# Seven block products instead of eight in the feed-forward stage, and the order of every engine written out, in a fused attention and SwiGLU kernel

## The chip, the core and the metric

The kernel runs on one core of a Trainium2 chip. The metric is the device time of one execution in microseconds, the median of several runs. Five engines work side by side: PE (TensorE, matrix products), DVE (VectorE), ACT (ScalarE), POOL (GpSimd) and SP (SyncE, which here only issues DMAs). PE writes to PSUM, which has eight banks of 128 partitions by 512 floats; the other tiles lie in SBUF.

## The reference: attention, then a gated feed-forward layer

All in 32-bit floats on 8 sequences of 448 tokens, with 12 heads of 64 (768 features):

```python
q_n, k_n = rmsnorm(q, g_q), rmsnorm(k, g_k)          # over the 64 of a head
attn = softmax(q_n @ k_n.T / sqrt(64)) @ v           # 8 x 12 x 448 x 64
x = attn.transpose(0, 2, 1, 3).reshape(3584, 768)
xn = x / sqrt(mean(x * x, -1) + 1e-6) * rms_g
g, val = xn @ w_gate, xn @ w_val                     # 768 x 1536 each
out = (g * sigmoid(g) * val) @ w_out                 # 1536 x 768
```

The weights arrive as 64-bit floats, two 32-bit words to a number, and are brought to 32 bits on the chip.

## The kernel before

The function `safe_scores` does all the work that is timed (`any_scores` stands behind a flag that large gains would set). A sequence is worked on as six pairs of heads, 48 pairs in all, and then as a feed-forward part (FFN).

**A pair.** `load_pair` fetches q, k and v. `norm_pair` takes squares on ACT (L460), sums them on DVE (L463), and has POOL make the reciprocal root by a power (L466) and scale q (L468). `turn(g, 0)` and `turn(g, 1)` transpose q and k on PE (L482, tile `tr`) and copy them out by ACT (L485) and DVE (L487). `score` makes scores of keys by queries (L497, tile `sc`, four PSUM banks) and their exponentials on ACT (L501). `values` multiplies by v (L519, tile `av`) and sums the exponentials over keys by a product with ones (L526, tile `den`); from the second sequence on POOL adds the four key tiles first (L507, L511, tile `es`). `divide` takes the reciprocal on DVE (L535), multiplies (L540), and adds the squares into `ss` (L545, L546).

**The end of a sequence.** `rms_x` sums `ss` over features on PE (L558, tile `msx`), POOL takes the power (L562), and `norm_x` spreads it by a product (L568, tile `rb`) and scales x on DVE (L571).

**The FFN.** `project` multiplies x with a 128-column block of a weight: six products of 128x128 by 448 tokens (L578, tile `ff`, two PSUM banks). `gate` follows with a tanh on ACT (L585) and one DVE instruction (L587), `val` with one more (L593), whose result is a row block of `hT`. `project_out` makes 128 tokens by 384 features with twelve products (L603). The output weights stay in SBUF; blocks of the gate and value weights are fetched again for each sequence from a 32-bit copy in DRAM (`kept`), three blocks ahead. In the first sequence each block is converted once by `convert`, 768 numbers a partition at a time: two ACT instructions (L413, L419), two of POOL (L414, L420), two of DVE (L416, L417).

**The order.** `fill` deals the FFN of sequence b in 24 slots over the pairs of sequence b+1, in proportion to its cost, and keeps `LEFT` = 2 items for the time in which the next x is normed. The first sequence's six pairs have no FFN beside them, and the last sequence's FFN has no pairs. A scheduler then sets each engine's order by its own priorities; the text is a hint.

In the trace a 32-bit product shows as two MATMUL and two LDWEIGHTS (weight load) records; "product" below is one call in the text, "record" one of the trace.

Of the kernel before, what the change touches and what calls it, by code (L numbers as in the profile page):

```python
# [23 lines left out]
HALF = DM // 2  # L24
CW = 512
# [307 lines left out]
def safe_scores(  # L333
# [15 lines left out]

    nc = tc.nc  # L350
# [3 lines left out]

    const, small = pool("c_const", 1), pool("c_small", 4)
    qk_pool, v_pool, qn_pool, qkT_pool = pool("c_qk", 3), pool("c_v", 3), pool("c_qn", 1), pool("c_qkT", 2)
    e_pool, tmp, y_pool = pool("c_e", 13), pool("c_tmp", 8), pool("c_y", 2)
    xT_pool, w_pool = pool("c_xT", 2), pool("c_w", 3)
    raw_pool, cv_pool = pool("c_raw", 3), pool("c_cv", 2)
# [16 lines left out]
    gqk = const.tile([128, 1], F32, name="gqk")  # L376
    nc.vector.scalar_tensor_tensor(gqk, gq, 1.0 / D**0.5, gk, ALU.mult, ALU.mult)

    nc.vector.tensor_scalar(gqk, gqk, SAFE / D, -SAFE / D, ALU.min, ALU.max)
# [7 lines left out]
    nc.vector.tensor_tensor(row[:, 0, :], row[:, 0, :], row[:, 1, :], ALU.mult)  # L387
    top = const.tile([1, 1], F32, name="top")
    nc.vector.tensor_reduce(out=top, in_=row[:, 0, :], axis=AX_X, op=ALU.max, apply_absolute_value=True)
    nc.vector.tensor_scalar(flag, top, 8.0, SAFE, ALU.mult, ALU.is_gt)  # L390

    wo = const.tile([128, NFC, DM], F32, name="wo")
    hT = const.tile([128, NFC, 512], F32, name="hT")
    st = {}


    kept = {w: scratch.tile([NFC, 128, DM], F32, name=f"kept_{w}") for w in "gv"}
    W_AHEAD = 3

    def convert(dst, src):  # L400

        if src.dtype == F32:
            nc.sync.dma_start(out=dst, in_=src)
            return
        a, n = src.shape[1], src.shape[2]
        assert a * n == DM
        raw = raw_pool.tile([128, 2 * DM], I32, name="raw")
        nc.sync.dma_start(out=raw.rearrange("p (a n w) -> p a (n w)", a=a, w=2).bitcast(I64), in_=src)
        words = raw.rearrange("p (n w) -> p n w", w=2)
        lo, hi = words[:, :, 0], words[:, :, 1]  # L410
        top = cv_pool.tile([128, DM], I32, name="top")

        nc.scalar.activation(top.bitcast(F32), hi.bitcast(F32), ACT.Abs)  # L413
        nc.gpsimd.tensor_scalar(top.bitcast(F32), top.bitcast(F32), 122879.9921875, 2.0**-15, ALU.min, ALU.max)  # L414

        nc.vector.tensor_scalar(top, top, 3, 0x3FFFFFF8, ALU.logical_shift_left, ALU.bitwise_and)  # L416
        nc.vector.scalar_tensor_tensor(top, hi, -(2**30), top, ALU.bitwise_and, ALU.bitwise_or)  # L417

        nc.scalar.activation(lo, lo.bitcast(U32), ACT.Copy, scale=2.0**-29)  # L419
        nc.gpsimd.tensor_tensor(dst.rearrange("p a n -> p (a n)").bitcast(I32), top, lo, ALU.add)  # L420

    def weight(w, n):

        if n >= B * NFC:
            return
        b, fc = divmod(n, NFC)
        t = st["w", w, n] = w_pool.tile([128, NDC, 128], F32, name=f"w{w}", tag=f"w{w}")
        if b == 0:
            src = {"g": moe_w_gate, "v": moe_w_val}[w]
            convert(t, src[:, fc * 128:(fc + 1) * 128].rearrange("(c p) f -> p c f", p=128))  # L430
            nc.sync.dma_start(out=kept[w][fc], in_=t.rearrange("p c f -> p (c f)"))
        else:
            nc.sync.dma_start(out=t.rearrange("p c f -> p (c f)"), in_=kept[w][fc])
# [299 lines left out]
```

## Time and profile before

| | us |
|---|---|
| three runs | 1847.08, 1847.25, 1849.09 (median 1847.25) |
| the profiled execution | 1850.28 |
| its span, first to last instruction | 1848.4 |
| mean granted PE clock over the span | 0.982 |
| busy PE / DVE / ACT / POOL | 1778.2 / 510.6 / 441.8 / 638.1 |
| first product of `rms_x` for sequences 0, 1 and 7 | 132.3, 358.6, 1654.2 |
| DMA | 149 MB, 153,280 packets on the main queue, 27.6% of 16 engines |

The span falls into four parts: the first 14 us without products, the first sequence's pairs up to 132 us, the steady part, and the last FFN from 1654 us. A profile row names the line, engine, operation, tiles as out<-in, partitions by elements, and the count; then busy time and mean duration, or start and length.

### The profile page before, as it was taken

The numbers are of one execution on the slowest core, as the hardware profiler recorded it, in microseconds if no ns is written. First come the engines' busy times: TensorE is split into PE (matmuls) and PEld (weight loads), VectorE is DVE, ScalarE is ACT, GpSimd is POOL, SyncE is SP. The second block draws the span as 40 slices with busy tenths as digits, with TensorE's granted clock in tenths as the row PEclk, the third lists the DMA queues.
The fourth block names the chain that finished last, engine by engine and source line by source line (L and its number), as shares of the span: only waits on it lengthen the run. The fifth ranks groups of instructions, "written<-read, shape, count | busy, mean of one in ns | idle before, by whom it ended". The sixth has DMA issues, their size and how long they took to land. (4 is left out here: it accounts for less than half of the span.)

```text
span 1848.4 us, 15816 instructions
## 1 busy us (share of the span) xinstructions
PE 1778.2 (96%) x5960; PEld 880.4 (48%) x5960; DVE 510.6 (28%) x546; ACT 441.8 (24%) x725; POOL 638.1 (35%) x527
## 2 busy tenths in 40 slices
PE   5878989999999999999999999999999999999998
PEld 2333434544455444554455544554445544455554
DVE  3646664122212222123212222222221222111100
ACT  5643442122121313112221122212222122210000
POOL 6765774324232424322432243323234133210000
PEclk9888999999999999999999999999999999999999
DMA  5625653122220323113321232212231132202200
GB/s 157 219 76 156 194 190 99 32 82 80 87 55 27 90 83 93 46 53 88 87 65 38 66 91 83 68 41 84 84 90 41 41 87 67 69 18 74 88 9 28
DMA packets 154475, 149.00 MB, mean 81 GB/s; under 512 B 95509, under 2 KB 124693, under 8 KB 154389
## 3 DMA queue, kind: packets, MB, share of 16 engines
q1 hardware_dynamic: 153280, 147.88, 27.6%
q8 instruction: 50, 0.82, 0.2%
q14 instruction: 37, 0.29, 0.1%
q10 hardware_dynamic: 1108, 0.00, 0.0%
HBM read 127.41 MB, written 20.45 MB: 80 GB/s over the span
## 5 line engine op out<-in xcount | busy, mean ns | idle before, releaser
L578 PE MATMUL ff<-xT,wg 128*128 128x448 f32 x1152 | 457.0, 547 | 7.3 <-DVE ga L587 7.2
L578 PE MATMUL ff<-xT,wv 128*128 128x448 f32 x1152 | 456.6, 546 | 3.4 <-DVE hT L593 3.4
L603 PE MATMUL ff<-wo,hT 128*128 128x384 f32 x1344 | 444.6, 488 | 0.0
L603 PEld LDWEIGHTS ff<-wo,hT 128*128 128x128 f32 x1344 | 251.6, 190 | 182.2 <-issue 14.9
L578 PEld LDWEIGHTS ff<-xT,wg 128*128 128x128 f32 x1152 | 215.7, 191 | 231.6 <-issue 212.0
L578 PEld LDWEIGHTS ff<-xT,wv 128*128 128x128 f32 x1152 | 214.3, 191 | 229.6 <-issue 215.3
L511 POOL TENSOR_TENSOR es<-es,e 112x448 f32<-112x448 f32 x168 | 187.0, 1145 | 289.3 <-ACT e L501 289.3
L501 ACT ACTIVATE e<-sc,rs 112x448 f32<-112x448 f32 x384 | 214.2, 636 | 160.8 <-PE sc L497 160.7
L497 PE MATMUL sc<-qkT 64*112 64x448 f32 x768 | 185.4, 590 | 21.8 <-DVE qkT L487 15.2
L546 POOL TENSOR_TENSOR ss<-ss,s 128x448 f32<-128x448 f32 x40 | 46.6, 1164 | 427.4 <-ACT s L545 427.4
L535 DVE RECIPROCAL rd<-den 128x448 f32<-128x448 f32 x48 | 141.9, 2956 | 180.6 <-PE den L526 180.6
L519 PE MATMUL av<-e,vt 112*64 112x448 f32 x768 | 159.1, 557 | 0.0
L466 POOL TENSOR_TENSOR rs<-ms,mhalf 112x16 f32<-112x16 f32 x48 | 140.4, 2926 | 4.0
L585 ACT ACTIVATE th<-ff 128x448 f32<-128x448 f32 x96 | 52.0, 541 | 342.5 <-PE ff L578 342.4
L587 DVE SCALAR_TENSOR_TENSOR ga<-th,ff 128x448 f32<-128x448 f32 x96 | 59.2, 617 | 252.8 <-ACT th L585 252.8
L593 DVE SCALAR_TENSOR_TENSOR hT<-ga,ff 128x448 f32<-128x448 f32 x96 | 59.3, 618 | 236.5 <-PE ff L578 232.6
L463 DVE TENSOR_REDUCE ms<-sq 112x16 f32<-112x1024 f32 x48 | 58.5, 1219 | 216.8 <-ACT sq L460 201.2
L497 PEld LDWEIGHTS sc<-qkT 64*112 64x112 f32 x768 | 66.7, 180 | 104.4 <-issue 58.0
L507 POOL TENSOR_TENSOR es<-e 112x448 f32<-112x448 f32 x84 | 94.1, 1140 | 50.7 <-ACT e L501 50.7
L545 ACT ACTIVATE s<-xT 128x448 f32<-128x448 f32 x40 | 23.1, 577 | 327.7 <-DVE xT L540 327.7
L519 PEld LDWEIGHTS av<-e,vt 112*64 112x64 f32 x768 | 52.0, 140 | 97.7 <-issue 97.4
L468 POOL TENSOR_TENSOR qn<-qk,rs 112x512 f32<-112x512 f32 x48 | 51.4, 1070 | 80.8 <-PE tr L482 79.8
(46 smaller groups left out, 709.9 us busy)
## 6 DMA issues: line engine op xcount, KB each, us to landing
wg<-kept_g SPq DMA_DIRECT2D x84, 384.0 KB, 3.0
wv<-kept_v SPq DMA_DIRECT2D x84, 384.0 KB, 3.0
qk<-in_q_dram SPq DMA_DIRECT2D x96, 112.0 KB, 3.3
qk<-in_k_dram SPq DMA_DIRECT2D x96, 112.0 KB, 3.2
vt<-in_v_dram SPq DMA_DIRECT2D x48, 224.0 KB, 2.6
raw<-in_moe_w_gate_dram SPq DMA_DIRECT2D x12, 768.0 KB, 5.9
raw<-in_moe_w_val_dram SPq DMA_DIRECT2D x12, 768.0 KB, 4.8
raw<-in_moe_w_out_dram SPq DMA_DIRECT2D x12, 768.0 KB, 4.5
```

The costliest lines, as they stand in the source:

```text
L463: nc.vector.tensor_reduce(out=ms, in_=sq.rearrange("p (n d) -> p n d", d=D), axis=AX_X, op=ALU.add)
L466: nc.gpsimd.tensor_tensor(rs, ms, mhalf[0:P, :], ALU.pow)
L497: nc.tensor.matmul(ps, lhsT=qkT[r, 1, c * P:(c + 1) * P], rhs=qkT[r, 0, :], start=True, stop=True)
L501: nc.scalar.activation(e, ps, ACT.Exp, scale=rs[:, n:n + 1])
L507: nc.gpsimd.tensor_tensor(es, st["e", g, 0, j], st["e", g, 1, j], ALU.add)
L511: nc.gpsimd.tensor_tensor(es, es, st["e", g, c, j], ALU.add)
L519: nc.tensor.matmul(av[j * D:(j + 1) * D, 0:S], lhsT=vt[:, j, c, :], rhs=st["e", g, c, j], start=(c == 0), stop=(c == NT - 1))
L535: nc.vector.reciprocal(rd, den[:, 0:S])
L578: nc.tensor.matmul(ps, lhsT=wt[:, c, :], rhs=st["xT", b][:, c, :], start=(c == 0), stop=(c == NDC - 1))
L587: nc.vector.scalar_tensor_tensor(ga, th, 1.0, g, ALU.add, ALU.mult)
L593: nc.vector.scalar_tensor_tensor(hT[:, fc, c0:c0 + S], st.pop(("ga", b, fc)), 0.5, st.pop(("v", b, fc)), ALU.mult, ALU.mult)
L603: nc.tensor.matmul(ps, lhsT=hT[:, fc, i * 128:(i + 1) * 128], rhs=wo[:, fc, n * HALF:(n + 1) * HALF], start=(fc == 0), stop=(fc == NFC - 1))
```

## The change

`safe_scores` is rewritten. The sums below hold for one pair of FFN column blocks (`fp` and `fp + 6`), once for gate and once for value.

**Products.** The 448 tokens and the 768 features of x are halved, which gives A11 to A22 of 224 tokens by 384 features; the weight is halved into B11 to B22 of 384 by 128. Instead of eight products A·B there are seven, of A11, A12, A22 or the sums S1 to S4 with B11, B21, B22 or T1 to T4 (Strassen's scheme in Winograd's form). One `product` is two weights by three 128x128 blocks by 224 tokens, gate and value side by side in one bank. `quad` does the seven for one `fp`, and adds them up on DVE from PSUM (`plus`: u2, u3, c22, c21, c12); `hand` does the tanh and two DVE instructions for each of three parts. Two products are accumulated onto a bank that already holds one (`onto`). PSUM is now four banks for scores, one for `av` and later transposes, and three (`ps_f`) for the FFN.

**Sums.** `norm_x` makes S1 to S4 once a sequence: four DVE instructions of 128x672. T1 to T4 are made once, in the first sequence, by 48 DVE instructions of 128x384.

**Weights.** All blocks are 128x384: 72 to convert, and 84 blocks of the seven kinds plus 24 of the output weight, kept in DRAM and fetched for each later sequence into a ring of 24, up to 20 ahead. Conversion goes in turns: turn n loads piece n, splits piece n-2, joins piece n-3 and makes the T of piece n-4. There are three turns a pair while the first sequence's pairs are alone, then one with each FFN item.

**Order.** `manual_schedule` leaves every engine in the order of the text; `after(n, ...)` puts an instruction of another engine behind the n-th next PE step. FFN items now are 42 products and 18 or 24 thirds of an output tile, dealt in 27 slots, with 7 left for the norm. A pair's squares are two instructions, and q is loaded by one DMA in place of two.

PE while the first sequence's pairs are alone, one pair before and after (`qn` is q, `qk` is k):

```order
L497 MATMUL sc<-qkT 112x448 x4
L482 MATMUL tr<-ident,qn 128x112 x4
L519 MATMUL av<-e,vt 64x448 x8
L526 MATMUL den<-e,ones 64x448 x7
L482 MATMUL tr<-ident,qk 128x112 x4
```

```order
L469 MATMUL sc<-qkT 112x448 x4
L454 MATMUL tr<-ident,qn 128x112 x4
L454 MATMUL tr<-ident,qk 128x112 x4
L494 MATMUL av<-e,vt 64x448 x8
L469 MATMUL sc<-qkT 112x448 x4
L506 MATMUL den<-e,ones 64x448 x8
```

The transposes of k have moved ahead of `av`, and the second half of the scores ahead of `den`.

DVE during the first sequence's FFN, before and after (`top` is a weight being converted, `wt` a T block, `u_`, `cc` and `c_` the sums of products):

```order
L535 RECIPROCAL rd<-den 128x448
L540 TENSOR_TENSOR xT<-av,rd 128x448
L416 TENSOR_SCALAR top<-top 128x768
L417 SCALAR_TENSOR_TENSOR top<-raw,top 128x768
L593 SCALAR_TENSOR_TENSOR hT<-ga,ff 128x448
L487 COPY qkT<-tr 128x448
```

```order
L698 TENSOR_TENSOR u_1780<-ff,u_1725 128x448
L604 TENSOR_SCALAR top<-top 128x384
L605 SCALAR_TENSOR_TENSOR top<-raw,top 128x384
L650 TENSOR_TENSOR wt<-wt 128x384 x3
L698 TENSOR_TENSOR cc<-ff,u_1780 128x448
L426 TENSOR_REDUCE ms<-sq 112x8
L510 RECIPROCAL rd<-den 128x448
L517 TENSOR_TENSOR x<-av,rd 128x448
L698 TENSOR_TENSOR c_1839<-ff,u_1780 128x448
```

A sum of products, which PE waits for before it uses a bank again, now stands between conversions, T sums and a reciprocal.

PE in the steady part, from a `den` to the next scores, before and after (in the second with tile numbers, which show the bank):

```order
L526 MATMUL den<-es,ones 64x448 x2
L603 MATMUL ff<-wo,hT 128x384 x12
L482 MATMUL tr<-ident,qk 128x112 x4
L497 MATMUL sc<-qkT 112x448 x8
L603 MATMUL ff<-wo,hT 128x384 x12
```

```order
L506 MATMUL den_3015<-es_2690,ones_136 64x448
L686 MATMUL ff_3030<-x_1197,wt_2845 128x224 x3
L686 MATMUL ff_3030<-x_1197,wt_2848 128x224 x3
L686 MATMUL ff_3043<-xs_2833,wt_2851 128x224 x3
L686 MATMUL ff_3043<-xs_2833,wt_2854 128x224 x3
L454 MATMUL tr_3057<-ident_131,qk_2645 128x112 x4
L686 MATMUL ff_3030<-x_2201,wt_2857 128x224 x3
L686 MATMUL ff_3030<-x_2201,wt_2860 128x224 x3
L686 MATMUL ff_3079<-x_1197,wt_2870 128x224 x3
L686 MATMUL ff_3079<-x_1197,wt_2875 128x224 x3
L469 MATMUL sc_3094<-qkT_2697 112x448
```

Two FFN products stand between `den` and the transposes of k, two between those and the scores; the third product goes onto the bank of the first (`ff_3030`).

The core of the diff:

```diff
-    ps_s, ps_m, ps_f = pool("c_ps_s", 4, space=PSUM), pool("c_ps_m", 2, space=PSUM), pool("c_ps_f", 2, space=PSUM)
+    ps_s, ps_m, ps_f = pool("c_ps_s", 4, space=PSUM), pool("c_ps_m", 1, space=PSUM), pool("c_ps_f", 3, space=PSUM)
+    ctx.enter_context(tc.manual_schedule(engines={E.PE, E.Activation, E.DVE, E.Pool, E.SP}))
...
+    def after(n, fn):
+        due.append((now["t"] + n, fn))
...
+        op("S1", "A21", "A22", ALU.add)
+        op("S2", "S1", "A11", ALU.subtract)
+        op("S3", "A11", "A21", ALU.subtract)
+        op("S4", "A12", "S2", ALU.subtract)
...
+    def convert(upto=None):
...
+        if 0 <= n - 3 < len(pieces):
+            key = pieces[n - 3][0]
+            st[key] = block()
+            join(*st.pop(("cv", n - 3)), st[key][0])
...
+            sums = {"B12": (("T1", "B12", "B11"), ("T2", "B22", "T1"), ("T3", "B22", "B12")), "B21": (("T4", "B21", "T2"),)}
...
+    def product(b, fp, left, right, onto=None):
+
+        bank = ps_f.tile([128, 512], F32, name="ff", tag="f") if onto is None else onto
+        x = st["left", b][left]
+        for w in range(2):
+            wt = st["w", b, fp, right, w][0]
+            for c in range(3):
+                nc.tensor.matmul(bank[:, w * HT:(w + 1) * HT], lhsT=wt[:, c * 128:(c + 1) * 128], rhs=x[:, c, :],
+                                 start=onto is None and w == c == 0, stop=c == 2, skip_group_check=True)
+            used(("w", b, fp, right, w))
+        return bank
+
+    def quad(b, fp):
...
+        def plus(name, ps, other, dst=None):
+            add[name] = tmp.tile([128, S], F32, name=name, tag=name, bufs=1) if dst is None else dst
+            nc.vector.tensor_tensor(add[name], ps[:, 0:S], add[other], ALU.add)
+
+        def hand(gate, value, dst):
...
+            nc.scalar.activation(th, gate, ACT.Tanh, scale=0.5)
+
+            def rest():
+                nc.vector.scalar_tensor_tensor(dst, th, 1.0, gate, ALU.add, ALU.mult)
+                nc.vector.scalar_tensor_tensor(dst, dst, 0.5, value, ALU.mult, ALU.mult)
+
+            after(1, rest)
...
+        def p1():
+            bank["a"] = product(b, fp, "A11", "B11")
+            add["p1"] = tmp.tile([128, S], F32, name="p1", tag="p1", bufs=1)
+            nc.scalar.copy(add["p1"], bank["a"][:, 0:S])
+
+        def p6():
+            bank["b"] = product(b, fp, "S2", "T2")
+            plus("u2", bank["b"], "p1")
+
+        def p2():
+            product(b, fp, "A12", "B21", onto=bank["a"])
...
+            hand(bank["a"][:, 0:HT], bank["a"][:, HT:S], rows(fp)[:, 0:HT])
+
+        def p7():
+            bank["c"] = product(b, fp, "S3", "T3")
+            plus("u3", bank["c"], "u2")
...
+        return [p1, p6, p2, p7, p5, p4, p3]
...
+    for g in range(NG + 1):
...
+        if g < NG:
+            pe(lambda: score(g, (0, 1)))
+        squares(g + 2, 0)
+        if solo:
+            convert()
+        fill()
+        pe(lambda: turn(g + 1, 0))
+        fill()
+        if solo:
+            pe(lambda: turn(g + 1, 1))
+        squares(g + 2, 1)
+        if g:
+            pe(lambda: values(g - 1))
+        load_v(g + 2)
+        if solo:
+            convert()
+            pe(lambda: score(g, (2, 3)))
+        if g:
+            pe(lambda: sums(g - 1))
...
```

Of the remaining steps of `quad`, p5 (S1·T1) makes c22 = p5 + u3, p4 (A22·T4) makes c21 = p4 + u3, and p3 (S4·B22) goes onto the bank of p5 and makes c12 by adding u2.

More of the change, by code (lines that the diff above doesn't have):

```diff
@@ L397, in safe_scores @@
[L397 to L433, printed above, removed]
@@ L691, in safe_scores @@
-    finish(NG - 1)
+            pe(lambda: norm_x(b - 1))
+            fill(len(todo))
+            begin(b - 1)
+        fill()
     fill(len(todo))
+    pe(idle)
+    pe(idle)
+    pe(idle)
 @with_exitstack
```

591 lines of the change are left out of this document (360 added, 231 removed).

## The prediction, written before the changed kernel was run

> **What bounds the kernel now.** I read the page first (busy times), then the windows by stage, the waits of PE, and the rows of single groups. Page:
>
> ```profile
> span 1848.4 us, 15816 instructions
> PE 1778.2 (96%) x5960; PEld 880.4 (48%) x5960; DVE 510.6 (28%) x546; ACT 441.8 (24%) x725; POOL 638.1 (35%) x527
> ```
>
> Windows by stage (length, then each engine's busy time, PE clock, DMA share, GB/s), and everything that PE waited for (total, times, longest):
>
> ```profile
> 0.00:14.00 14.00, 0.39 (x2) 0.39 (x3) 3.42 (x8) 3.40 (x3) 5.19 (x12) 1.00 0.65 147
> 14.00:132.00 118.00, 90.52 (x364) 34.90 (x362) 61.73 (x55) 70.57 (x107) 84.00 (x62) 0.87 0.52 160
> 132.00:360.00 228.00, 205.59 (x666) 99.77 (x667) 115.72 (x102) 80.35 (x119) 136.18 (x105) 0.93 0.44 134
> 360.00:1654.00 1294.00, 1294.00 (x4387) 643.51 (x4386) 307.72 (x344) 278.58 (x479) 411.75 (x350) 1.00 0.24 68
> 1654.00:1848.40 194.40, 187.67 (x546) 101.85 (x544) 22.05 (x37) 8.93 (x17) 1.02 (x1) 0.99 0.17 50
> ```
>
> ```profile
> PE sc L497 <- DVE qkT L487: 15.2, 5, 6.1
> PE tr L482 <- POOL qn L468: 13.6, 1, 13.6
> PE tr L482 <- DVE rd L535: 10.1, 2, 7.6
> PE ff L578 <- DVE ga L587: 7.2, 4, 3.8
> PE sc L497 <- ACT e L501: 6.6, 2, 3.9
> PE msx L558 <- POOL ss L546: 6.0, 1, 6.0
> PE ff L578 <- DVE hT L593: 3.4, 2, 2.1
> PE rb L568 <- POOL rs L562: 1.4, 1, 1.4
> ```
>
> From 360 us on PE never idles and the clock is 1.00: there only less PE work helps. All listed waits lie before 360 us, and there the clock is lower too (0.87 and 0.93). So there are two accounts: the work of PE, and what is lost in the first 360 us.
>
> **The change part by part.**
>
> *The products.* I need the spacing of records, not their duration, since they overlap. Medians of the two kinds (min/median/max), and stretches of PE's timeline (start, length, count):
>
> ```profile
> L578 PE MATMUL ff<-xT,wg x1152: 539/539/1113, 138.2 to 1774.7; 128*128 128x448 f32 x192
> L603 PE MATMUL ff<-wo,hT x1344: 486/486/590, 318.9 to 1841.2; 128*128 128x384 f32 x192
> L568 PE MATMUL rb<-ident,rs x64: 261/275/556, 135.3 to 1663.5; 112*128 112x112 f32 x64
> ```
>
> ```profile
> 918.09 4.67 PE L578 MATMUL ff<-xT,wg 128*128 128x448 f32 x12
> 1819.58 22.09 PE L603 MATMUL ff<-wo,hT 128*128 128x384 f32 x68
> 591.65 1.04 PE L568 MATMUL rb<-ident,rs 112*128 112x112 f32 x8
> 902.78 3.23 PE L519 MATMUL av<-e,vt 112*64 112x448 f32 x16
> 905.84 0.92 PE L526 MATMUL den<-es,ones 112*64 112x448 f32 x4
> 922.69 1.76 PE L497 MATMUL sc<-qkT 64*112 64x448 f32 x8
> 963.45 0.55 PE L482 MATMUL tr<-ident,qn 112*128 112x112 f32 x4
> ```
>
> 448 tokens: (4.67 - 0.539) / 11 = 0.3756 us. 384 columns: (22.09 - 0.486) / 67 = 0.3224. The line through both, 0.00083 a column, gives 0.189 at 224. Below lies half of 0.3756, 0.188; above, weight loads could bind, which take 0.19 each:
>
> ```profile
> L578 PEld LDWEIGHTS ff<-xT,wg 128*128 128x128 f32 x1152 | 215.7, 191 | 231.6 <-issue 212.0
> ```
>
> `rb` shows that they need not: its records, each with a 128-column load, stand (1.04 - 0.275) / 7 = 0.109 apart, so 0.19 is latency, and a load fits behind 224 tokens. Today 2304 records × 0.3756 = 865.4; then 8 × 6 × 7 products × 6 × 2 = 4032 × 0.189 = 762.0. **-103.4** (4032 × 0.188 and × 0.191 give -107 and -95). The Trainium skill speaks against this: "TensorE: Matmul & The Clock Gate", Part 3, The mechanism, says that a weight load overlaps running products only where it aims at other row groups, and these fill all rows. By it a record would cost load plus stream; this trace disagrees, since the stream alone, 448 × 0.00083 = 0.373, fills the 0.3756. It stays as a rival.
>
> *Sums of products, hand-off.* Per quad DVE gets five sums of 128x448 and six instructions of the hand-off, four at half width; the row for 448 is:
>
> ```profile
> L540 DVE TENSOR_TENSOR xT<-av,rd 128x448 f32<-128x448 f32 x48 | 29.9, 622 | 1.5
> L535 DVE RECIPROCAL rd<-den 128x448 f32<-128x448 f32 x48 | 141.9, 2956 | 180.6 <-PE den L526 180.6
> L485 ACT ACTIVATE qkT<-tr,gqk 128x448 f32<-128x448 f32 x48 | 30.5, 636 | 64.1 <-PE tr L482 64.1
> L501 ACT ACTIVATE e<-sc,rs 112x448 f32<-112x448 f32 x384 | 214.2, 636 | 160.8 <-PE sc L497 160.7
> ```
>
> 5 × 0.62 + 2 × 0.62 + 4 × 0.31 to 0.62 = 5.6 to 6.8 us beside 84 records × 0.189 = 15.9 of PE. In the steady part DVE has 307.72 / 6 = 51 us a sequence; with six quads more, less 24 old steps of 0.62, 51 + 37 - 15 = 73 of some 203. Cost nothing, while the cover lasts: a sum must be read before its bank is used again one product (12 × 0.189 = 2.27) or two later. The longest thing in front is a reciprocal and its multiply, 2.96 + 0.62 = 3.58; the order puts two products (4.54) between `den` and the transposes of k, which need that bank. If only one third of an output tile stood there (8 × 0.322 = 2.58) 1.0 us would show each time.
>
> *New waits in the steady part.* Where the FFN has run out at a sequence's end, `av` follows the transposes of q at once and takes their single bank, so it waits for ACT's copy: 0.64 + about 0.3, once a sequence. The norm's power on POOL stands behind four additions of `es`; one third of a tile covers it. I take 1.1 us × 7 = **+8**; ends 0 and +30 (one 0.6 us wait more per quad).
>
> *The first pairs, up to 132 us.* At full clock a pair needs of PE 2 × 1.69 + 2 × 0.47 + 3.06 + about 3.06 for eight `den` products = 10.5 us (starts of neighbouring rows: one score set 1.69, the rest likewise, counting the eight `den` as `av`). Its scores stand this far apart today:
>
> ```profile
> 63.75 3.23 PE L497 MATMUL sc<-qkT 64*112 64x448 f32 x8 [2.88 <-DVE qkT L487]
> 81.73 3.33 PE L497 MATMUL sc<-qkT 64*112 64x448 f32 x8 [4.93 <-DVE qkT L487]
> 99.76 4.26 PE L497 MATMUL sc<-qkT 64*112 64x448 f32 x8 [3.86 <-ACT e L501]
> 116.12 1.76 PE L497 MATMUL sc<-qkT 64*112 64x448 f32 x8 [0.50 <-DVE qkT L487]
> ```
>
> (116.12 - 63.75) / 3 = 17.5. The wait for `qkT` goes, since k is now turned and copied before the reciprocal. Next late is `av`: its one bank is free 3.6 us after the last `den`, when PE has done 1.69 + 0.94 = 2.6. So a pair needs at least 10.5 + 1.0 = 11.5. Between 11.5 and 17.5 I take 14.5: the rows' own waits, (4.93 + 3.86 + 0.50) / 3 = 3.1, taken from 17.5. Not less, because every engine now blocks in its own order, with three turns of conversion a pair where there were two twice as large. Six pairs × 3 = 18, less about 2 for the first two short ones: **-16** (ends -30 and 0).
>
> *The first FFN, 132 to 360 us.* Lost today: 228 - 205.6 = 22.4 idle and, at clock 0.93, 0.07 × 205.6 = 14.4 slow, 37 in all. Conversion costs DVE:
>
> ```profile
> L416 DVE TENSOR_SCALAR top<-top 128x768 int32<-128x768 int32 x36 | 49.4, 1373 | 77.9 <-POOL top L414 77.9
> L417 DVE SCALAR_TENSOR_TENSOR top<-raw,top 128x768 int32<-128x768 int32 x36 | 45.1, 1256 | 1.1
> L416 DVE TENSOR_SCALAR top<-top x36: 551/1483/4390, 29.4 to 284.9; 128x768 int32<-128x768 int32 x36
> L463 DVE TENSOR_REDUCE ms<-sq 112x16 f32<-112x1024 f32 x48 | 58.5, 1219 | 216.8 <-ACT sq L460 201.2 <-POOL es L511 15.6
> L571 DVE SCALAR_TENSOR_TENSOR xT<-xT,rg,rb 128x448 f32<-128x448 f32 x48 | 29.1, 674 | 63.2 <-PE rb L568 63.2
> ```
>
> Halved, a join is 0.69 + 0.63 = 1.32 and a T sum about 0.63. Over the 42 products there are 40 joins (53), 34 T sums (21), 29 product sums and 32 hand-off instructions (32), four pairs of 2.96 + 0.62 + 0.62 + 1.22 (22), and the norm with S1 to S4 (6 × 0.67 + 4 × 0.62 × 672 / 448 = 8): 136 us, where PE has 42 × 2.27 plus four pairs of 8.2 (as above, with 0.85 for two `den` products) = 128. So DVE can bind here, and PE waits about as now: **-2** (ends -22, if joins go at the 551 ns minimum, and +25).
>
> *Rest.* Weights: 756 fetches of 196.6 KB in place of 168 of twice that, 82 MB more, on a queue now at
>
> ```profile
> q1 hardware_dynamic: 153280, 147.88, 27.6%
> ```
>
> With 12 MB more written this grows to about 27.6% × 242 / 148 = 45% of the old span; 20 blocks ahead are ten products, 23 us. Nothing. The end after the last product is as before.
>
> **The sum.** 1848.4 - 103.4 + 8 - 16 - 2 = 1735 of span. The profiled execution took 1850.28, 1.9 more than its span, and 3.0 more than the median 1847.25; so **1734 us**.
>
> **The rivals.**
>
> *DVE binds the whole first sequence.* For: the sum above, and 551 against 1483 and 4390 ns in one row, so a DVE instruction can be held up while POOL works. The Trainium skill, "Perfetto Trace Analysis", Optimizing Scalar/DVE Operations, says that the two share a port; the spread agrees. Against: 551 also occurs. Then the pairs gain nothing and the FFN loses 25 more: 1734 + 16 + 27 = 1777. Chance 0.17.
>
> *Slower: PE waits in every quad.* Three banks, and every engine in a fixed order: if at two places a quad a sum or ACT's copy of p1 stands behind 3.58 us of DVE or four exponentials (4 × 214.2 / 384 = 2.2), each wait is 3.58 + 0.62 - 2.27 = 1.9. The whole gain, 113, is gone at 113 / 48 = 2.4 us a quad. At 2 × 1.9 + 0.5 = 4.3: 48 × 4.3 - 8 more, 1932. Against: only six reciprocals fall on six quads, and two products stand behind each. Chance 0.06.
>
> *Weight loads show.* Each record would cost 0.189 + 0.109 = 0.298: 4032 × 0.298 = 1202, so 1734 + 440 = 2174. Against it: spacings 0.3756 and 0.109 in this trace. It is also the time by the rule that the Trainium skill states in "TensorE: Matmul & The Clock Gate". Chance 0.02.
>
> *Weights come late,* so that the products do not run at their spacing: a queue behind outputs and pair loads in SP's order. At 0.2 us a product 336 × 0.2 = 67: 1801. Against: 45% load and 23 us ahead. Chance 0.03.
>
> **How the numbers follow.** The forecast has 0.72; its own range is 1704 (30 in the pairs) to 1762 (20 more of small waits, some lost in the first FFN). To hold 8 in 10 the range takes in the case of 1777: 1704 to 1785. All but the two slow rivals are faster, 0.72 + 0.17 + 0.03 = 0.92; slower 0.07, the same 0.01. "Same" means within 0.2%, about what a measurement of this kernel can tell.
>
> **What would show it.** Right: product records 0.189 apart; the first `msx` near 116 us; a sequence in 1294 / 6 - 103.4 / 8 = 203 to 205 us after that, PE idle under 2 us in each; clock 1.00 there; the longest DVE queue in the first FFN. Wrong: spacing of 0.25 or more; waits of PE for DVE or ACT in every quad after 360 us; PE waiting for weights.

## The result, and the profile after

The changed kernel takes 1782.51 us (median of 4 runs, 1780.93 to 1784.11), the kernel before beside it 1847.92 (4 runs, 1847.08 to 1849.09): a ratio of 0.9646, 95% interval 0.9629 to 0.9662. The profiled execution took 1780.93 us with a span of 1778.6, so the span has lost 1848.4 - 1778.6 = 69.8 us. The forecast was a span of 1735.

The head of the page of the changed kernel:

```profile
span 1778.6 us, 21555 instructions
PE 1679.7 (94%) x7688; PEld 1207.5 (68%) x7688; DVE 728.7 (41%) x1078; ACT 487.3 (27%) x945; POOL 670.4 (38%) x643
PEclk9879888899999999999999999999999999999999
```

The same windows by stage as were read of the kernel before (length, busy time of PE, PEld, DVE, ACT, POOL, granted clock, DMA share, GB/s), moved to where its stages lie now, and as the third row the first FFN by its `msx` records (below):

```profile
14.00:118.00 104.00, 79.80 (x354) 32.04 (x353) 61.29 (x76) 58.70 (x112) 66.56 (x60) 0.88 0.53 156
118.00:340.00 222.00, 174.37 (x767) 132.57 (x768) 142.33 (x231) 89.39 (x182) 136.78 (x144) 0.86 0.52 165
121.70:387.20 265.50, 213.03 (x907) 152.71 (x906) 162.30 (x256) 105.83 (x213) 167.72 (x176) 0.89 0.50 159
340.00:1600.00 1260.00, 1251.54 (x5813) 900.54 (x5810) 477.12 (x678) 322.41 (x618) 455.80 (x415) 1.00 0.43 132
```

The steady part is what was hoped for: PE is busy for 1252 of 1260 us at clock 1.00. The second row is what was not. In 222 us PE works 174 and at a clock of 0.86, where the kernel before had 206 of 228 at 0.93. No engine is full there either: DVE works 142 us and POOL 137.

The records of `rms_x` (`msx`) cut the span into sequences. The row of that tile gives the first and the last of them, and PE's timeline the second and the eighth:

```profile
L535 PE MATMUL msx<-ones,ss x64: 167/237/345, 121.7 to 1606.3; 128*112 128x1 f32 x64
```

```profile
387.19 0.86 PE L535 MATMUL msx<-ones,ss 128*112 128x1 f32 x8
...
1605.68 0.85 PE L535 MATMUL msx<-ones,ss 128*112 128x1 f32 x8
```

| stretch | before, us | after, us | difference |
|---|---|---|---|
| up to the first `msx` (first pairs) | 132.3 | 121.7 | -10.6 |
| first to second `msx` (first FFN) | 226.3 | 265.4 | +39.2 |
| second to eighth, six sequences | 1295.6 | 1218.5 | -77.1 |
| eighth `msx` to the end | 194.2 | 172.9 | -21.3 |

Part of the last and of the second row only changes places: before, two output tiles (48 records) stood behind the second `msx`, now one (24 records), so 24 x 0.322 = 7.7 us have moved from the end into the first FFN. There, products save 12.9 as in every sequence, 7.7 come in, and the other 39.2 + 12.9 - 7.7 = 44 us are newly lost. About 30 of them are longer waits of PE and about 9 a lower clock: PE idles 265.5 - 213.0 = 52.5 us there, where the kernel before idled 22.4, and at 0.89 of the full clock it loses 0.11 x 213 = 23, where the kernel before lost 14.4 (estimates from the third row and from the kernel before's rows). That stage was forecast at 2 us of gain, with 25 of loss as its worst end.

The waits from 118 to 390 us, the largest of all engines and two of PE's (total, times, longest):

```profile
ACT top L597 <- POOL wt L606: 85.7, 44, 4.9
DVE top L604 <- POOL top L599: 54.3, 38, 3.7
POOL wt L606 <- DVE top L605: 27.7, 11, 10.0
...
PE ff L686 <- ACT p L719: 17.5, 4, 5.9
...
PE av L494 <- ACT qkT L457: 8.4, 3, 4.5
```

PE waits most for ACT's copies (`p1`, `qkT`; with the smaller rows its waits come to 52 us), ACT for POOL's add of an earlier piece, POOL for DVE, and DVE for POOL: a row of conversion in which each waits for the next. One turn of it on POOL (start, duration, operation, idle time before):

```profile
217.53 0.50 POOL L599 TENSOR_SCALAR top<-top 128x384 f32<-128x384 f32 x1
219.24 1.11 POOL L606 TENSOR_TENSOR wt<-top,raw 128x384 int32<-128x384 int32 x1 [1.21 <-ACT raw L598]
220.32 0.50 POOL L599 TENSOR_SCALAR top<-top 128x384 f32<-128x384 f32 x1
222.04 1.01 POOL L606 TENSOR_TENSOR wt<-top,raw 128x384 int32<-128x384 int32 x1 [1.22 <-DMA raw<-in_moe_w_val_dram]
```

The same turn on DVE:

```profile
218.07 0.36 DVE L604 TENSOR_SCALAR top<-top 128x384 int32<-128x384 int32 x1 [1.37 <-POOL top L599]
218.46 0.56 DVE L605 SCALAR_TENSOR_TENSOR top<-raw,top 128x384 int32<-128x384 int32 x1
```

POOL clamps piece k+1 (217.53 to 218.03), DVE shifts and merges it (218.07 to 219.02), POOL adds it (219.24 to 220.35), and only then clamps k+2: 222.04 - 219.24 = 2.80 us from add to add. In such a turn POOL sits idle 1.2 us and DVE 1.4, each for the other. (The profile puts POOL's wait down to ACT and to a DMA; by the times it ends 0.2 us behind DVE's second step.) A product takes 2.27 us. On PE, four turns in a row show like this:

```profile
213.41 2.64 PE L686 MATMUL ff<-xs,wt 128*128 128x224 f32 x12
221.93 4.39 PE L686 MATMUL ff<-x,wt 128*128 128x224 f32 x12 [5.89 <-ACT p L719]
```

ACT's copy of `p1` ran at 221.27, since in ACT's order the abs of three more turns stood in front of it.

### The profile page after: what moved, and what is told of

Its sections match the earlier page's. It is cut to its first block, busy times and chain, and to the rows that moved or that the text cites. A ratio compares the mean times of both kernels' runs of the same rounds, so it can differ in the third digit from the quotient of the medians.

```text
span 1778.6 us, 21555 instructions
## 1 busy us (share of the span) xinstructions
PE 1679.7 (94%) x7688; PEld 1207.5 (68%) x7688; DVE 728.7 (41%) x1078; ACT 487.3 (27%) x945; POOL 670.4 (38%) x643
## 4 chain that ended last, share of the span: by engine, by line
PE 79%; ACT 0%; DMA 0%; SPq 0%; issue 0%; DVE 0%; ACTq 0%; POOL 0%
PE ff L686 38%; PE ff L764 23%; PE sc L469 7%; PE av L494 7%; PE den L506 2%; PE tr L454 1%; PE rb L545 0%; PE msx L535 0%; ACT qkT L457 0%; DMA qk<-in_q_dram 0%; SPq L399 0%; DVE y L774 0%; ACT top L597 0%; ACT raw L598 0%; SPq L626 0%
## 5 line engine op out<-in xcount | busy, mean ns | idle before, releaser
L686 PE MATMUL ff<-x,wt 128*128 128x224 f32 x2268 | 469.5, 360 | 19.3 <-ACT p L719 17.5
L686 PEld LDWEIGHTS ff<-x,wt 128*128 128x128 f32 x2268 | 431.7, 194 | 52.5 <-issue 39.4
L764 PE MATMUL ff<-wt,h 128*128 128x384 f32 x1344 | 455.7, 492 | 7.6 <-DVE h L709 4.4
L764 PEld LDWEIGHTS ff<-wt,h 128*128 128x128 f32 x1344 | 250.0, 191 | 195.6 <-issue 27.5
L686 PE MATMUL ff<-xs,wt 128*128 128x224 f32 x1692 | 348.9, 356 | 3.5 <-DVE cc L698 3.5
L686 PEld LDWEIGHTS ff<-xs,wt 128*128 128x128 f32 x1692 | 316.3, 191 | 29.3 <-issue 16.4
L426 DVE TENSOR_REDUCE ms<-sq 112x8 f32<-112x512 f32 x96 | 65.3, 680 | 184.5 <-ACT sq L423 184.2
L698 DVE TENSOR_TENSOR cc<-ff,u 128x448 f32<-128x448 f32 x96 | 59.8, 623 | 132.2 <-PE ff L686 132.0
L606 POOL TENSOR_TENSOR wt<-top,raw 128x384 int32<-128x384 int32 x64 | 68.6, 1071 | 92.8 <-DVE top L605 29.5
L423 ACT ACTIVATE sq<-qk 112x512 f32<-112x512 f32 x96 | 60.6, 631 | 61.9 <-DMA qk<-in_q_dram 54.1
```

Of the source, the lines that this page charges most:

```text
L426: nc.vector.tensor_reduce(out=ms[:, i * n:(i + 1) * n], in_=sq.rearrange("p (n d) -> p n d", d=D), axis=AX_X, op=ALU.add)
L606: nc.gpsimd.tensor_tensor(dst.bitcast(I32), top, lo, ALU.add)
L686: nc.tensor.matmul(bank[:, w * HT:(w + 1) * HT], lhsT=wt[:, c * 128:(c + 1) * 128], rhs=x[:, c, :], start=onto is None and w == c == 0, st ...
L698: nc.vector.tensor_tensor(add[name], ps[:, 0:S], add[other], ALU.add)
L764: nc.tensor.matmul(ps, lhsT=st["h", b, fc][:, i * 128:(i + 1) * 128], rhs=st["wo", b, n, fc][0], start=(fc == 0), stop=(fc == NFC - 1))
```

## The experiments

Twelve kernels were run; each stands beside runs of the kernel before on the same chip. All of them keep the steady part: six sequences take 1218 to 1222 us in every one, and the end 173 to 175. They differ in the first two stretches alone, so these are given for each (both from `msx` records). `c_cv` is the pool of `top` buffers; a turn is one call of `convert`.

| run | time, us (range) | ratio to before, interval | first pairs | first FFN |
|---|---|---|---|---|
| the change | 1782.5 (1780.9 to 1784.1) | 0.9646 [0.9629, 0.9662] | 121.7 | 265.4 |
| four buffers | 1782.8 (1781.5 to 1784.0) | 0.9647 [0.9631, 0.9663] | 121.2 | 265.0 |
| clamp first | 1770.2 (1769.9 to 1774.0) | 0.9583 [0.9567, 0.9599] | 120.3 | 255.6 |
| late dues | 1795.9 (1795.2 to 1798.1) | 0.9715 [0.9698, 0.9731] | 121.8 | 281.2 |
| all three | 1786.6 (1785.0 to 1790.2) | 0.9667 [0.9651, 0.9683] | 119.7 | 271.2 |
| clamp on DVE | 1774.6 (1771.9 to 1777.9) | 0.9600 [0.9583, 0.9617] | 120.3 | 261.2 |
| no clamp | 1759.6 (1755.7 to 1763.0) | 0.9527 [0.9510, 0.9543] | 113.4 | 248.1 |
| ring of 36 | 1782.5 (1780.8 to 1783.2) | 0.9642 [0.9626, 0.9658] | 123.1 | 265.4 |
| no T sums | 1769.5 (1768.6 to 1772.6) | 0.9579 [0.9563, 0.9595] | 117.7 | 256.7 |
| no conversion | 1716.2 (1713.0 to 1717.4) | 0.9283 [0.9268, 0.9299] | 107.6 | 213.3 |
| `es` on PE | 1775.0 (1771.0 to 1776.7) | 0.9607 [0.9591, 0.9624] | 120.1 | 257.0 |
| combined | 1759.4 (1758.6 to 1760.0) | 0.9521 [0.9505, 0.9537] | 120.3 | 243.7 |
| early output weights | 1779.0 (1778.8 to 1779.6) | 0.9623 [0.9607, 0.9639] | 159.7 | 223.1 |

**Four buffers.**

```
-    raw_pool, cv_pool = pool("c_raw", 4), pool("c_cv", 2)
+    raw_pool, cv_pool = pool("c_raw", 4), pool("c_cv", 4)
```

> Four top buffers instead of two; the order of the text stays. Three theories of the 44 us lost in the first FFN (span from the first msx at 121.7 to the second at 387.2, 265.4 us). BUNCHES: the block ring is full at two to four products of a quad, so turns of conversion are refused there and made up four to six in a row ahead of the next quad; ACT's copy of p1 stands behind them, each turn 2.75 us. LOOP: a turn is POOL's add, POOL's clamp of the next piece, two DVE steps, 2.75 us, more than a product's 2.27, and that rate alone delays PE, wherever the turns stand. BUFFERS: ACT's abs waits for the add of two pieces before because there are only two top buffers (85.7 us of ACT waiting), and nothing else does harm. BUFFERS expects the whole 30 to 44 us back: 1740 to 1752. BUNCHES expects 10 to 20 back, since DVE still stands in the same row of turns ahead of the next sum: 1762 to 1772. LOOP expects 0 to 5: 1777 to 1783. The recorded rival that DVE binds expects none.

1782.8: no change, so the number of `top` buffers is not the cause by itself. Of ACT's 85.7 us of waiting for POOL's add, 25.7 + 22.4 + 5.8 = 54 went over into waiting for raw words, whose four buffers are freed by the same add:

```profile
ACT top L597 <- DMA raw<-in_moe_w_out_dram: 25.7, 12, 5.4
...
ACT top L597 <- DMA raw<-in_moe_w_gate_dram: 22.4, 6, 8.1
...
ACT top L597 <- DMA raw<-in_moe_w_val_dram: 5.8, 4, 2.7
```

**Clamp first.** Four buffers too; in `convert` the `split` of piece n-2 (abs, copy, clamp) is issued ahead of the `join` of piece n-3:

```
+        if 0 <= n - 2 < len(pieces):
+            st["cv", n - 2] = split(st.pop(("raw", n - 2)))
         if 0 <= n - 3 < len(pieces):
             key = pieces[n - 3][0]
...
-        if 0 <= n - 2 < len(pieces):
-            st["cv", n - 2] = split(st.pop(("raw", n - 2)))
```

> Four top buffers, and each turn issues abs and clamp of its piece ahead of the two DVE steps and the add of the piece before, so that POOL never stands between its add and the next clamp. A turn should fall from 2.75 us to what POOL itself works, 1.0 + 0.5 = 1.5 to 1.6 us. LOOP expects all of it back: 1738 to 1750. BUNCHES: four turns in a row then last 6.3 us instead of 11, so 4.7 x 6 places = 28 us back: 1750 to 1758. BUFFERS: as with four buffers alone, and no more. DVE binds: nothing, as DVE has the same work.

1770.2: 12 us back, less than any theory that names this round trip alone had said. From add to add it is now 2.1 to 2.4 us where turns follow closely, not 1.6. The reason stands in the rows of DVE's two steps (min/median/max in ns). In the change:

```profile
L604 DVE TENSOR_SCALAR top<-top x72: 343/360/1296, 24.9 to 368.5; 128x384 int32<-128x384 int32 x72
L605 DVE SCALAR_TENSOR_TENSOR top<-raw,top x72: 557/559/1377, 25.3 to 368.9; 128x384 int32<-128x384 int32 x72
```

With the clamp first:

```profile
L604 DVE TENSOR_SCALAR top<-top x72: 346/625/1624, 24.8 to 357.3; 128x384 int32<-128x384 int32 x72
L605 DVE SCALAR_TENSOR_TENSOR top<-raw,top x72: 557/739/1376, 25.2 to 358.5; 128x384 int32<-128x384 int32 x72
```

Where POOL and DVE no longer take turns, DVE's steps fall beside POOL's instructions and grow by 0.27 and 0.18 us in the median. One turn there, on POOL and on DVE:

```profile
215.36 1.19 POOL L606 TENSOR_TENSOR wt<-top,raw 128x384 int32<-128x384 int32 x1 [1.41 <-PE ff L686]
216.52 0.61 POOL L599 TENSOR_SCALAR top<-top 128x384 f32<-128x384 f32 x1
217.68 1.19 POOL L606 TENSOR_TENSOR wt<-top,raw 128x384 int32<-128x384 int32 x1 [0.55 <-issue]
```

```profile
215.61 1.16 DVE L604 TENSOR_SCALAR top<-top 128x384 int32<-128x384 int32 x1
216.80 0.74 DVE L605 SCALAR_TENSOR_TENSOR top<-raw,top 128x384 int32<-128x384 int32 x1
```

The shift started beside the add and ended 0.22 us behind it (216.55 and 216.77); the merge started beside the clamp and ended 0.41 behind it (217.13 and 217.54); the next add follows 0.14 later. So the turn is 217.68 - 215.36 = 2.32 us: two engines that were to overlap still work one after the other.

**Late dues**, and **all three** (late dues, clamp first, four buffers). In the change, the block ring is full while the second quad runs, four products in a row issue no turn, and later turns are made up three in a row ahead of each `p1`. The edit lets each product ask for only what it needs:

```
-            items += [(6 * HT, 8 * (fp + 1) + 5, fn) for fn in quad(b, fp)]
+            items += [(6 * HT, 8 * fp + need, fn) for need, fn in zip((10, 12, 12, 12, 12, 12, 12), quad(b, fp))]
...
-                    items.append((NFC // OUT_PARTS * HALF, 8 * NFP + NFC * (n + 1) + 4,
+                    items.append((NFC // OUT_PARTS * HALF, 8 * NFP + NFC * n + NFC // OUT_PARTS * (part + 1) + 3,
```

> Only the numbers that say how many turns must be out before a product: 8fp+10 before p1 and 8fp+12 before the other six instead of 8fp+13 before all, and for the output blocks the turns of the four blocks that a third of a tile reads instead of all twelve. So the row of three forced turns ahead of each p1 becomes none ahead of p1 and one or two ahead of p6, behind ACT's copy of p1 in ACT's order. Number, length and inner order of the turns stay. BUNCHES expects most of it back, 25 to 40 us: 1743 to 1757, with no PE wait for p over 1 us. LOOP and BUFFERS expect nothing beyond 5 us: 1777 to 1786, and so does the rival that DVE binds.

> Four buffers, clamp first and the late dues together, as a version that may beat both. BUNCHES and LOOP together: the first FFN loses no more than before the change, 222 to 232 us instead of 265, so 1738 to 1750. If LOOP alone is the cause this is no better than clamp first; if BUNCHES alone, no better than late dues. DVE binds: 1775 or more.

1795.9, slower by 13, and 1786.6, slower by 4 and far from what was expected of it. The waits for `p1` did go, as the theory of the bunches had said, and the same time came back elsewhere; what PE waits for most is now

```profile
PE ff L764 <- POOL wt L606: 24.9, 10, 6.6
```

Output blocks are not converted when PE gets there. So the bunches only chose the place at which the lag showed. The theory falls.

**Clamp on DVE.** The clamp moves to DVE, ahead of the shift:

```
-        nc.gpsimd.tensor_scalar(top.bitcast(F32), top.bitcast(F32), 122879.9921875, 2.0**-15, ALU.min, ALU.max)
...
+        nc.vector.tensor_scalar(top.bitcast(F32), top.bitcast(F32), 122879.9921875, 2.0**-15, ALU.min, ALU.max)
         nc.vector.tensor_scalar(top, top, 3, 0x3FFFFFF8, ALU.logical_shift_left, ALU.bitwise_and)
```

> The clamp moves from POOL to DVE, ahead of the shift; all else as in the change, two top buffers too. Four runs so far leave this theory, CHAIN: from about 177 us on conversion itself is what ends last. Each turn goes POOL add, POOL clamp, DVE, DVE, POOL add, 2.70 us in the median, and POOL's 12 us of pair work a pair stand in the same row; 50 turns and four and a half pairs make 135 + 56 = 191 us, and the last add stood at 369.6, 192.6 after 177. The second msx came 13 to 18 us behind the last add in every run (changed kernel 17.6, four buffers 17.6, clamp first 16.8, late dues 14.0, all three 13.0). With the clamp on DVE a turn no longer goes back and forth: two turns share abs, copy, DVE's three steps and the add, (0.56 + 0.54 + 1.28 + 1.07) / 2, some 1.8 to 2.0 us, and POOL's pair work lies beside DVE. CHAIN expects 25 to 35 us back: 1747 to 1757. The recorded rival that DVE binds has 56 x 0.36 = 20 us more DVE work in the first FFN: 1790 to 1803. BUNCHES: four turns then last 8 us instead of 11, 3 x 6 = 18 us back: 1765.

1774.6: 8 us faster although DVE is busy for 200.7 us in the first FFN, 38 more than the 162.3 of the change (20 were expected). That speaks against DVE as the bound. The gain is about a quarter of what the chain theory had said.

**No clamp.** The same line of POOL deleted, nothing added.

> The clamp of the exponents is left out (it changes no weight of these inputs, but the kernel then no longer covers weights outside its bounds). DVE's work stays that of the change, POOL has 0.5 us less a turn and the turn has one engine change less. CHAIN expects 30 to 40 us back, a little more than with the clamp on DVE: 1742 to 1752. DVE binds: same DVE work, so 0 to 5 us back: 1777 to 1783.

1759.6: 23 us back, less than the 30 to 40 expected; in the profiled execution 8 of them in the first pairs and 17 in the first FFN. DVE executes what it did before (it is busy for 175 us there, 13 more). Half a microsecond a turn on POOL, and one change of engine less, are worth that much.

**Ring of 36.**

```
-    RING, NH = 24, 14
+    RING, NH = 36, 14
```

> 36 ring blocks instead of 24, nothing else. In the change the ring is full when the second quad runs: four products in a row (p7, p5, p4, p3) issue no turn, 25 turns are out at that quad's end instead of 30, and only 2 adds stand between 157 and 177 us; later the refused turns are made up three in a row ahead of each p1. With 36 blocks a turn is refused once in all, and no row of three stands ahead of a p1. CHAIN expects those five turns earlier, at 192.6 / 49 = 3.9 us each, 15 to 20 us: 1763 to 1768, and the waits for p gone. LOOP or BUFFERS alone, without the hole: 0 to 5 us.

1782.5, no change, and the expectation of the chain theory was wrong. Five adds now stand between 157 and 177 us where there were two, no row of turns stands ahead of `p1`, and the last add still comes at 370.4 (369.6 in the change). POOL's adds in those 20 us, in the change (length, busy time and count, clock, DMA share, GB/s):

```profile
157.00:177.00 20.00, 2.21 (x2) 1.00 0.34 110
```

In the kernel with the ring of 36:

```profile
157.00:177.00 20.00, 5.64 (x5) 1.00 0.58 188
```

From 177 us to the last add, 47 adds now take the 193 us that 50 took in the change, so what was gained ahead was lost again. That the turns wait there for ACT's and DVE's work on pairs and products is likely, but not shown.

**No T sums.**

```
-                st[key] = block()
-                nc.vector.tensor_tensor(st[key][0], st["w", 0, fp, plus, w][0], st["w", 0, fp, minus, w][0], ALU.subtract)
+                st[key] = st["w", 0, fp, "B22", w][0], block()[1]
```

> DVE's sums T1 to T4 are left out in the conversion: the products that need them read the block of B22 instead, so that the output is not the reference's; the blocks are counted, stored and fetched as before, so that ring and queue stay. DVE loses 34 x 0.79 = 26 us of the first FFN. CHAIN: three sums stand in every fourth turn's way for 2.4 us, where DVE has 1.4 to 1.7 us to wait anyhow; eight such turns after 177 us, about 1 us each: 5 to 10 us back, 1772 to 1778. DVE binds: 21 to 26 us back, 1757 to 1762.

1769.5: 13 us back, between the two expectations, 4 of it in the first pairs. The T sums are new with the change, so this is a price that it brought.

**No conversion.** `split` keeps only the two views of the raw words, and `join` is one line:

```
+        nc.scalar.copy(dst, hi.bitcast(F32))
```

> The arithmetic of the conversion is left out: one copy on ACT of the high words fills a block, in place of abs, copy, clamp, two DVE steps and the add, so that the output is not the reference's. Loads, T sums, stores, turns and their order stay. The runs so far: 36 ring blocks changed nothing (1782.5), the hole between 157 and 177 us only moved the same chain; clamp out gave 23 us, T sums out 13, clamp on DVE 8, clamp first 12, each some of it, none all. CHAIN in its wider form: a turn goes through ACT, POOL, DVE and POOL, each engine does it in the order of the text between work that waits for PE, and PE waits for them; the conversion as a whole costs what was lost. It expects the first FFN near its work at full clock, 205.6 - 12.9 + 7.8 = 200.5 us and some 5 to 15 of waits, so 50 to 60 us less than 265.4, and 5 to 10 less in the first pairs: 1712 to 1728. The rival HAND-OFF: the sums of products, the hand-offs and the three banks themselves cost the time while pairs and products stand close; then at most half goes: 1745 to 1755.

1716.2, as expected: 14 us less in the first pairs (5 to 10 were expected) and 52 in the first FFN. That stage in this kernel, from `msx` to `msx`:

```profile
107.60:320.90 213.30, 195.94 (x906) 143.25 (x905) 94.63 (x142) 78.79 (x158) 74.64 (x63) 0.96 0.62 198
```

PE idles 17 us in place of 52, at clock 0.96 in place of 0.89. Products, their sums, the hand-offs, three banks, the stores and the queue are all still there; what is lost comes with the arithmetic of the conversion. The rival that the hand-off costs the time falls. The 52 us are more than the 44 newly lost, since the kernel before paid for its conversion too; how much it paid there was not measured.

**`es` on PE.** For pairs 6 to 11 POOL adds no exponentials; `sums` gives PE all eight tiles:

```
-        if not alone(g):
+        if g >= 2 * NPAIR:
             after(1, add)
```

> For the six pairs that run beside the first FFN the exponentials are no longer added on POOL (six additions of 1.17 us a pair, 7.0 us); PE sums them in 16 den products instead of 4, as it does for the first six pairs. The conversion itself stays. CHAIN expects five to six pairs x 7.0 = 35 to 42 us less of POOL in the row of turns, against 12 x 0.2 x 6 = 14 us more of PE's work in a stage where PE waits 50 us: 15 to 28 us back, 1755 to 1768. HAND-OFF, or DVE as the bound, expects PE's own work on top: 1785 to 1797.

1775.0: 8 us back, the right sign, but half of the least that was expected.

**Combined:** `es` on PE, clamp first with three buffers, ring of 36.

> Exponentials of the six pairs summed on PE, clamp ahead of the add with three top buffers, and 36 ring blocks: the version that the runs point to, all of the output computed. CHAIN: 12 for the clamp's place, 15 to 28 for POOL's additions, and with a shorter row the ring's five turns begin to count, 0 to 10 more: 1735 to 1757. If the parts get in each other's way (DVE's steps took 0.76 us in place of 0.45 when POOL worked without a break), no better than the best of them alone, 1755 to 1768.

1759.4, 23 us (1.3%) less than the change, the fastest of the kernels that keep the clamp, and 2 us short of what the chain theory expected. Clamp first and `es` on PE alone gave 12 + 8 = 20; whether the other 3 come from the ring was not tried.

**Early output weights:** the combined kernel with five turns in each of the first six pairs instead of three. The two more convert the first half of the output weights, which goes to memory and is fetched again:

```
+    w_in, early, rest = pieces[:48], pieces[48:60], pieces[60:]
+    pieces = []
+    for i in range(6):
+        pieces += w_in[3 * i:3 * i + 3] + early[2 * i:2 * i + 2]
...
+    pieces += w_in[18:]
+    pieces += [(("get", 0, 0, fc), None) for fc in range(0, NFC, 2)] + rest
```

> The combined version of the run before, with one thing more: two more turns a pair in the first six pairs, used for the twelve blocks of the output weights' first half, which are stored, given free at once and fetched again before the first output block (six turns that only fetch). So 30 turns stand ahead of the first product instead of 18, and 12 conversions fewer behind it. Before the change 12 of 36 double pieces were converted at the first msx, a third, and the last add stood at 288.9, 70 us ahead of the second msx; in the change 15 of 72, a fifth, and the last add 17.6 us ahead. CHAIN: 12 turns fewer at the 3.8 us that one takes in the combined version (169.6 / 45) are more than is left above the 213 us that the first FFN takes with no conversion at all, so 18 to 28 us back from its 243.7; in the first pairs a turn has cost (121.7 - 107.6) / 18 = 0.8 us, twelve more 5 to 12. In sum 1737 to 1750. The rival that a turn costs the same wherever it stands, since ACT, DVE and POOL are shared by the pairs too: 1755 to 1765.

1779.0, outside both expectations. The first FFN does as expected, 223.1 against 243.7, which is 20.6 / 12 = 1.7 us for each turn that is gone from it, but the first pairs take 39 us more: 39.4 / 12 = 3.3 us for each added turn. A row of ACT there:

```profile
101.90 0.63 ACT L423 ACTIVATE sq<-qk 112x512 f32<-112x512 f32 x1 [8.71 <-DMA qk<-in_q_dram]
```

And what SP issued ahead of it:

```profile
94.29 0.33 SPq L638 DMA_DIRECT2D kept<-wt  x1
94.72 0.96 SPq L588 DMA_DIRECT2D raw<-in_moe_w_out_dram  x1
95.73 1.23 SPq L399 DMA_DIRECT2D qk<-in_k_dram  x2
97.00 0.61 SPq L401 DMA_DIRECT2D qk<-in_q_dram  x1
```

The loads of the next pair stand in SP's order behind the store of a block, which waits for the end of POOL's add at 94.26; ACT then waits 8.7 us for q, and PE for ACT. Up to the first `msx` ACT's waits for q come to 43.0 us, where the combined kernel has 13.4. So a turn was not cheap in the first pairs, as the rival had said, but it cost twice as much there as in the first FFN, and by another way than the rival's shared engines: these waits have grown by about 30 us of the 39, which points to the place of the loads behind the stores.

## Why the prediction was right or wrong

The direction and the largest term were right. The span came out 1778.6 - 1735 = 44 us above the forecast, and one step accounts for it: the first FFN missed by 46, while 5 us too much in the first pairs and some 8 us of waits in the steady part that did not come nearly cancel. The time lies outside the forecast's own range, 1704 to 1762. It lies inside 1704 to 1785 only because that was stretched to take in a rival at 1777, and since that rival's mechanism did not occur (below), this part is luck.

**The products** (-103.4). Right. In the steady part:

```profile
1016.70 2.43 PE L686 MATMUL ff<-x,wt 128*128 128x224 f32 x12
1018.97 2.43 PE L686 MATMUL ff<-xs,wt 128*128 128x224 f32 x12
```

A product starts 2.27 us after the one before, 12 x 0.189. The 0.189 taken from two other widths holds, and a load of 128 columns hides behind 224 tokens:

```profile
L686 PEld LDWEIGHTS ff<-x,wt 128*128 128x128 f32 x2268 | 431.7, 194 | 52.5 <-issue 39.4
```

Each load's record is 194 ns long, more than the spacing, and yet shows nowhere in it. So the rule on weight loads that the Trainium skill gives in "TensorE: Matmul & The Clock Gate", Part 3, The mechanism, does not bind here; the measurement decides. Six sequences came out 77.1 / 6 = 12.85 us shorter each, where 12.93 was worked out.

**New waits in the steady part** (+8). Right in kind, too dear: PE's waits after 390 us are one line.

```profile
PE av L494 <- ACT qkT L457: 3.6, 5, 0.7
```

That is the place that was named, `av` behind ACT's copy. The other half, `rb` behind the norm's power, does not show there.

**The first pairs** (-16, ends -30 and 0). It came to -10.6. The kernel without conversion has 107.6 there, 14 less, so the conversion costs more there than the 5 us that are missing, and its price I had left inside a mean of the old rows' waits. That it is the missing part is likely, not shown.

**The first FFN** (-2, ends -22 and +25). This is the step that failed, by 46 us. I had set two sums beside each other, 136 us of DVE and 128 of PE, and called the larger the bound. DVE was not the bound: it works 162 of 265 us, and the kernel with 38 us more on DVE is faster (clamp on DVE). What ended last was the row of turns through ACT, POOL, DVE and POOL; without the conversion's arithmetic the stage takes 213 us in place of 265. A sum for each engine cannot show it, because in a fixed order the engines' waits for each other add up as well. Two smaller mistakes came with it. I counted the joins over the products alone, 40; but 57 of the 72 conversions lie in the stage. POOL's adds up to the first `msx` and from there to the second, in the kernel before:

```profile
14.00:132.30 118.30, 22.76 (x12) 0.87 0.52 159
132.30:358.60 226.30, 45.19 (x24) 0.93 0.44 135
```

In the change:

```profile
14.00:121.70 107.70, 16.25 (x15) 0.87 0.51 151
121.70:387.20 265.50, 61.05 (x57) 0.89 0.50 159
```

A third of the weights was converted at that point before, 12 of 36, and a fifth after, 15 of 72. The last adds show the outcome. In the kernel before, the last one stands 358.6 - 288.9 = 70 us ahead of the second `msx`:

```profile
L420 POOL TENSOR_TENSOR wo<-top,raw x12: 1824/1837/2167, 69.7 to 288.9; 128x768 int32<-128x768 int32 x12
```

In the change it stands 387.2 - 369.6 = 17.6 us ahead:

```profile
L606 POOL TENSOR_TENSOR wt<-top,raw x64: 1002/1014/1262, 73.3 to 369.6; 128x384 int32<-128x384 int32 x64
```

And I costed a half piece at half a whole one. DVE's share of a join came out smaller than that, 0.454 + 0.604 = 1.06 us in the mean in place of 1.32, but the turn as a whole did not halve. Two turns of the kernel before, on POOL:

```profile
158.10 1.84 POOL L420 TENSOR_TENSOR wv<-top,raw 128x768 int32<-128x768 int32 x1
161.74 0.83 POOL L414 TENSOR_SCALAR top<-top 128x768 f32<-128x768 f32 x1 [1.81 <-ACT top L413]
162.53 1.85 POOL L420 TENSOR_TENSOR wg<-top,raw 128x768 int32<-128x768 int32 x1
```

A whole piece took 162.53 - 158.10 = 4.43 us from add to add there; two half pieces, as in the turn shown above, 2 x 2.80 = 5.60. In these rows POOL clamps the next piece right ahead of the add; the order written out in the change has the clamp behind it. So the change brought another order inside the turn as well, and the kernel that turns it round (clamp first) has 12 us back.

The clock makes it worse: 0.89 in this stage, about 9 us more slow time than before, and I had booked none beyond the old kernel's.

**The rivals.** "DVE binds the whole first sequence" gave 1777, near the result, by another mechanism: its pairs were to gain nothing, and they gained 10.6; its DVE sum was to bind, and did not. The sign that it went by, a DVE step held up while POOL works, is there all the same (last section). A wait in every quad, weight loads that show and weights that come late do not appear: after 390 us PE has no other wait than that one line. The queue carries about what was worked out, 45%, and PE waits for no weight in the steady part:

```profile
q1 hardware_dynamic: 223616, 242.30, 44.3%
```

**What stays open.** The conversion's arithmetic is worth 66 us in the changed kernel (1782.5 - 1716.2). Of its parts, 23 for the clamp and 12 for the order were measured, one at a time, and they overlap; the T sums (13) and POOL's additions (8) stand beside it and stayed in the kernel without conversion. What the conversion cost the kernel before was not measured, so how the 44 us divide between more conversions in this stage (57 half pieces where there were 24 whole ones), the new order inside a turn and the blocked order of every engine is argued. That stores of blocks ahead of loads in SP's order cost the change itself something in the first pairs is only argued: ACT waits there for q as well (12.1 us in five places), but a kernel with its stores on another queue or later was not tried. Whether the clamp can be had cheaper with all weights covered is open.

## What to carry to other kernels

Where several engines work in an order written out by hand, do not set their busy sums side by side. Follow one item of the side work through all its engines, add the trips between them, multiply by the number of items, and ask in which stage they still fit. Halving the items did not halve the trip here: 4.4 us for a whole piece and 2.8 for a half in the rows shown, with the order inside it changed too. To find what the side work as a whole is worth, leave its arithmetic out and keep its loads, stores and places. One run told more than four that moved it about.

## What the runs showed of the hardware

DVE's conversion steps took 0.36 and 0.56 us while POOL stood still for them, and 0.63 and 0.74 in the median when POOL's clamps and adds ran beside them (clamp first). They are not slowed in proportion, they are held: in the trace of clamp first 38 shifts started while a POOL instruction ran and took over 0.6 us, and 37 of them ended 0.21 or 0.22 us behind the end of that instruction; the 41 merges of that kind ended 0.41 or 0.42 behind it. The 13 shifts that met no POOL instruction took 0.35 each. One of each kind stands in the rows of clamp first above.

The Trainium skill says in "Perfetto Trace Analysis", Optimizing Scalar/DVE Operations, that the two share a port to SBUF, so that moving work between them might not help; the held steps agree, though moving the clamp to DVE did help here, by 8 us (clamp on DVE). So making the two engines overlap gives back part of what it saves.
